# Attention weights of three batches transposed by VectorE and DMA instead of TensorE, in a fused attention and channel-mix kernel

## The chip, the cores and the metric

One core of a Trainium2 chip runs the whole program. The metric is the time of one execution on the device in microseconds. The kernel before took 440.34 us in the median of three runs, 440.08 to 441.02.

## What is computed

Sparse attention for 4 batches, 8 heads, 768 tokens and 64 features a head, and on its output a channel mix with a sigmoid gate. Each query sees the keys less than 16 tokens away and 24 summaries of 32 tokens each (maximum of the keys, mean of the values). Cut to what matters:

```
k_sum = k.reshape(B, H, nb, block, D).max(axis=3)
v_sum = v.reshape(B, H, nb, block, D).mean(axis=3)
scores_l = scale * q @ k.T, kept where |i - j| < 16
scores_s = scale * q @ k_sum.T + log(32)
a = softmax(concatenate([scores_l, scores_s]))
x = a @ concatenate([v, v_sum])

xk = mu_k * x + (1 - mu_k) * x_prev      # x_prev: x one token earlier
xr = mu_r * x + (1 - mu_r) * x_prev
out = sigmoid(xr @ w_r) * (relu(xk @ w_k) ** 2 @ w_v)
```

## The kernel before

Attention is cut into 32 units: a batch, one of four pairs of heads, and one half (`hf`) of the 768 tokens. `unit` (L515) plans one. TensorE (PE) makes the scores for each window of 64 queries against 96 keys and 24 summaries, 120 columns (L529). VectorE (DVE) adds the mask and finds the extreme (L539), ScalarE (ACT) takes the exponential (L543), and the rows are divided by their sums on ACT, DVE or GpSimd (POOL) (L560, L554, L565). The weights then stand with queries on the partitions, in tiles `y` of 128 x 3 x 120, one for each head of the pair. The product with the values needs them the other way round, with keys on the partitions. So PE transposes each tile with three instructions into the PSUM tile `pt` (L577), and ACT or DVE copies it into a tile `pts` of SBUF (L583, L585). The values follow on PE (L592), and ACT or DVE copies the result into `vx` (L607, L606).

The channel mix of a batch and half makes the two mixed inputs (L625 to L638), each split into a high and a low part, then the gate on PE (L679 to L681), and for each of eight slices of the hidden layer a first product (L708), rectified and squared (L714, L716, L718), and a second one (L733; the last slice is L759). The expert work of one batch is the long part on PE; the units of the next batch run among it. Batch 0's units have no such work beside them and stand at the start, with the loading and unpacking of the weights (L354 to L402). In the waits of the start PE multiplies zeros into a spare corner (L809).

All loads and stores are issued by SyncE (SP), in order: an issue that waits for its operands holds up all that stand behind it. Among them are the tokens of a batch for the means of its values (L420, into the tiles `st`, of which there are three, which the packed weights use too), the spreading of these means into the value tiles (L510), the queries (L518), keys (L439), values (L444) and the stores (L769).

What stands where is set by a table: `op` records every operation with the engines that could do it, what it reads and writes and an estimate of its length (`LENGTH`, L41). `ORDER` (L72) lists the operations by number, some with a letter for another engine than the first (D for DVE, A for ACT, P for POOL). `schedule` (L207) walks the table, gives each operation a buffer of its pool and an estimated start. Each engine runs its operations in that order. From the estimated starts comes the number of products of zeros. The buffers that matter here:

```
y=tiles("y", 4, [P, NSL, NK]), mn=tiles("mn", 4, [P, NSL]), sm=tiles("sm", 3, [P, 2 * NSL]),
rc=tiles("rc", 3, [P, 2 * NSL]), pts=tiles("pts", 2, [NK, NSL, P]),
...
st=tiles("st", 3, [P, 1024], U32), wc=tiles("wc", 4, [P, 512], U32),
sc=tiles("sc", 2, [P, NSL, P], pool=psum), pt=tiles("pt", 1, [P, 512], pool=psum),
```

A unit uses two `y`, two `pts`, and the one `pt` twice.

Of the kernel before, what the change touches and what calls it, by code (L numbers as in the profile page):

```python
# [21 lines left out]
P = 128  # L22
NPAIR = H // 2
NS = S // BLOCK
QW = 64
# [24 lines left out]
    wcast_p=650, mixa_p=560, kcopy_p=400, spread_p=800, norm3_p=1100, tiny=60, vzero=800, vzero_d=480,  # L50
# [13 lines left out]
MIX_PE = ()  # L64
NORM = "DVE", "POOL"
# [7 lines left out]
1 4 5 229 2 13 14 181 0 34 7 206 28 16 15 17 19 18 47 20 3 21P 53 182 72 231 35 36 189 191 193 185 190 186 194 38 37  # L73
187 183 39 40P 256 55 54 8 9 207 192 188 184 10 281 74 195 11P 214 216 210 212 196 218 29 217 198 30 208 31 197D 6 12
201 22 97 85 209 211 215 219 32D 23 202D 48 49P 204 24 213 199 50 25 220 200 221 26 279 56 51 222 57 203 52 223 58 76
75 224 59P 232 205A 33 225 377 77 226 305 241 78P 233 243 242 73 27 239 237 235 41 400D 66 378 257 401 244 238 234 240
42 236 227 43 44 264 268 402D 379D 260 266 262 269 245 246 258 45 60 261 267 247D 228 259 61 263 265 248D 380 403 249
230A 404P 254 282 250D 270 381 62 353 624 590 271 287 251 63 272D 393 64 65 291 289 252D 285 283 293 98 273 288 86 290
382 405 87 99 383 88 406D 384 253 276 294 79 286 255A 385D 407 100 292 306 80 277 81 329 284 274 82 394 295 67 1034
121 591 109 317 307 83 315 275 68P 311 313 296 309 308 408 298 386 278 297D 387 299 101 330 69 388 594 300 409 280A  # L80
301 648 91 650 599 89 316 318 314 310 335 336 339 333 337 331 395 389P 341 302 412P 410 312 110 390 70D 391D 354 71
303 392 413 396 90 111 414 332 122 415 411 340 338 319 102 416 112 320 123 103 321D 397 399 398 124 323 421 322D 133
# [12 lines left out]
766 1092 655 714 523D 524 525A 691 531 1039 1025 526 1040 822D 716 646 673 695 1043 677 738 719 678D 536 675 770 721
717 1095 534 537 693 1096 723 718 647A 725 844D 724 685 689 923 726 538 727 535 532 676D 696D 697 699D 741 924 679
1026 771 798 1030 1150 713 772 702 541 533 557 542 728 720 703 752 722 750 845 748 681 539A 925 729 846D 698 926 1029
823 730 700 558 824 559 701 548 742 744 746 747 745 749 774 704 1068 1151 743 826 751 825 731D 733 734 753 540 777
1153 775 732 1031 827 550 549 735 551 776 1154 785 552 754 555 564 778 736 1155 779 781 755 828D 756 560A 847 783 561
553 780 705A 757 829 784 782 758 737 739A 759D 1097 799 760 556 808 806 761 802 565D 804 810 809 786 787 566 807 803  # L100
562 852P 554 1035 563 800 853 788 1027 789P 854D 805 848P 811 567 801 790 1044 762 791 569 1045 830P 792 763A 793 570
1047 812 813 814D 855 1046 794 1049 1055 568 831 832D 815 795 797A 834 835 1051 1053 1050 818 849 836D 819 1052 577
574 571 816 1069 817 1048 820 833 837 575 1032 1070 1071 1033 1076 931D 850D 856 1074 1080 1072 578 1073 1081 1054
1056 1057 1077 1075 1078 572 857 1079 1082 1058 838 839 1059 1098 932 1060 858D 821 1101 1159 475 1094 1470 1478 576
840 842 1126 573 579 1480 1041 1468 1157 1594 1093 1036 1061 1062 1100 1474 1102 1063 841 851 859 927P 1064 843 1083
1085 1113 865 860 861 866 867 868A 862 1103 935D 1156 1469 936 1084D 1107 937D 938 1105 1111 928 1109 1086 1065 1127
1087D 863A 933 1597 1130 1088 879 1134 1136 1598 864 1099 1184 1536 1135 1106 1067 1114 1108 1110 1042 1472 1217 1132
934 869 880D 870 871 872 1540 1138 945D 1128 946 1089 1471 1539 873 874 877 1131 1112 929D 875 881 957 1137 1104 1139
876 930 1541 878 886 887D 884 1124 1133 1129 958 1115 1599 888 1140D 882 883 1116 1473 1482 953D 900 889A 1117 1118
1600 1481 1160 1090 901 1119 885 939 1161 1162 1120 1121 891 940 1167 1165 1475 890 892 893 898 954 1169 1163 894D 902  # L110
895 896 1171 1542 1141 1143 1122 1483 899 941 905 1142 903A 1091A 942 943 947D 904 959 955 956 960 944 1185 1123 1208
1210 948 897 1144 1152 1158 1242 1479 907 949 1145 950 951D 1192 952 1196 908 906 1146 961 1186 1194 1166 909 1197
1147 910A 1168 1125 1193 1270D 912 1182 1292 1271 1172 962D 963 911 980 913 1188 1272D 1187 1170 1212 1273 1293 1190
1191 1164 1484 1211 917 920 1173 1174 1213 1148 1214P 981D 1176D 1175D 918 1218 1189 982 964A 965 1476 1066 914 1195
1477 1486 1177 973 1178 915 1537 1216 1179 966 987 1225 983 1227 1219 921 1221 1603 1180 1222 1294 974D 1149A 1220
1228 1229 1230 1198 1223 984 1199 1201D 1200D 1243 1181 1487 1652 967 968 1224 975 1202 971 1209 916 919 1248 1203D
1204 969 972 1254 1246 1244 978 1226 1252 970 1245 1247 1255 988 1183A 1296D 1205D 979 1655 976A 1001 1231D 977 1232
# [139 lines left out]
def tile_kernel(ctx: ExitStack, tc: tile.TileContext, q, k, vT, v, fixed, w_k, w_v, w_r, out):  # L257
# [150 lines left out]
    def windows(vw):  # L408
        return vw.t[0:NK, 0:S].rearrange("p (w d) -> p w d", d=P)
# [498 lines left out]
```

## Time and profile before

| | |
|---|---|
| median of three runs | 440.34 us (440.08 to 441.02) |
| span of the profiled execution | 438.2 us; the page has no time of its own beside it |
| PE busy | 431.6 us, 3568 matmul records |
| VectorE busy | 295.4 us |
| ScalarE busy | 277.9 us |
| GpSimd busy | 31.1 us |
| DMA | 51.71 MB, 118 GB/s over the span |

The span is the time from the first to the last instruction of one execution; the time of a run has some more around it. Busy time of PE is modelled from records of pipelined instructions: two that follow each other overlap, so the sum of their durations is longer than the path through them. The chain of waits is a path through the run, followed back from the last instruction, and its pieces add up without overlap; what is on it has delayed the end. A stretch is a window of time counted from the start of the span. "SPq" is the queue of SyncE, on which a DMA is issued.

### The profile page before, as it was taken

The page shows a single profiled execution, that of the slowest core. Times are in us where ns is not written, and L with a number is a line of the kernel's source. Part 1 is how long each engine was busy: PE and PEld are TensorE (multiplying, and loading weights), DVE is VectorE, ACT ScalarE, POOL GpSimd, SP SyncE. Part 2 cuts the span into 40 slices and gives each one's busy share as a digit, 9 for nine tenths or more (in the row PEclk, how much of TensorE's full clock was granted, in tenths as well). Part 3 has the DMA queues.
Part 4 walks back from the last instruction along what each step waited for, and adds up shares of the span by engine and source line. Part 5 has one row for each costly group of instructions (what it writes and reads, how often), then busy time and mean ns, then how long its engine had stood idle before and what let it go on. Part 6 is the DMA issues. An engine that isn't in the chain of part 4 may idle for free.

```text
span 438.2 us, 9571 instructions
## 1 busy us (share of the span) xinstructions
PE 431.6 (99%) x3568; PEld 374.1 (85%) x3568; DVE 295.4 (67%) x961; ACT 277.9 (63%) x839; POOL 31.1 (7%) x69
## 2 busy tenths in 40 slices
PE   9999999999999999999999999999999999999996
PEld 8877988788887889889888888888888889889985
DVE  5999999998977877537667857456355754444121
ACT  4999999875998878557655767757445433223211
POOL 3322220100002000000010000000100000000000
PEclk9999999999999999999999999999999999999999
DMA  8979479457533584005361312102100010002003
GB/s 298 401 283 344 115 252 357 145 210 221 155 120 97 204 240 125 1 1 184 87 204 38 104 34 68 43 0 85 56 0 2 2 48 0 1 0 73 0 1 120
DMA packets 26878, 51.71 MB, mean 118 GB/s; under 512 B 2640, under 2 KB 14544, under 8 KB 26832
## 3 DMA queue, kind: packets, MB, share of 16 engines
q1 hardware_dynamic: 26832, 51.10, 35.2%
q8 instruction: 28, 0.46, 0.5%
q14 instruction: 18, 0.15, 0.1%
HBM read 43.03 MB, written 6.29 MB: 113 GB/s over the span
## 4 chain that ended last, share of the span: by engine, by line
PE 80%; ACT 7%; DMA 5%; DVE 4%; SPq 1%; issue 1%; DVEq 0%
PE mm L708 27%; PE mm L733 24%; PE av L592 5%; PE pt L577 4%; PE mm L681 4%; PE mm L680 4%; PE mm L679 4%; PE sc L529 4%; PE mm L759 4%; DMA st<-in_w_k 3%; DMA kt<-in_k 2%; ACT wc L361 2%; ACT y L543 1%; DVE y L539 1%; ACT L693 1%
## 5 line engine op out<-in xcount | busy, mean ns | idle before, releaser
L708 PE MATMUL mm<-xs,wk_h 128*128 128x384 f32 x512 | 101.9, 340 | 0.0
L708 PEld LDWEIGHTS mm<-xs,wk_h 128*128 128x128 f32 x512 | 90.0, 188 | 3.9 <-ACT r L714 0.3
L543 ACT ACTIVATE y<-y,mn 128x120 f32<-128x120 f32 x192 | 74.1, 388 | 20.7 <-DVE mn L539 20.3
L733 PE MATMUL mm<-wv_h,kh 128*128 128x512 f32 x168 | 67.4, 401 | 0.0
L733 PE MATMUL mm<-wv_l,kh 128*128 128x512 f32 x168 | 66.0, 393 | 0.0
L539 DVE CUSTOM_DVE_ANT_0 y<-sc,mask_sb 128x120 f32<-128x120 f32 x192 | 46.8, 275 | 22.0 <-PE pt L577 17.6
L718 ACT ACTIVATE r<-r 128x384 f32<-128x384 f32 x64 | 33.1, 521 | 40.9 <-DVE r L716 40.4
L708 PE MATMUL mm<-xs,wk_l 128*128 128x384 f32 x256 | 54.7, 334 | 0.0
L733 PE MATMUL mm<-wv_h,kl 128*128 128x512 f32 x168 | 48.7, 398 | 0.0
L708 PEld LDWEIGHTS mm<-xs,wk_l 128*128 128x128 f32 x256 | 45.3, 188 | 0.0
L723 DVE TENSOR_TENSOR kl<-r,kh 128x384 fp32r<-128x384 f32 x64 | 35.2, 553 | 14.4 <-ACT kh L722 12.2
L632 DVE SCALAR_TENSOR_TENSOR xa<-vx,fixed_sb,xa 128x384 f32<-128x384 f32 x64 | 39.1, 615 | 4.0 <-ACT xa L625 3.9
L638 DVE TENSOR_TENSOR xs<-xa,xs 128x384 fp32r<-128x384 f32 x64 | 34.4, 552 | 7.3 <-ACT xs L635 5.0
L679 PE MATMUL mm<-wr_h,xs 128*128 128x512 f32 x96 | 38.3, 399 | 0.0
L681 PE MATMUL mm<-wr_h,xs 128*128 128x512 f32 x96 | 37.6, 391 | 0.0
L680 PE MATMUL mm<-wr_l,xs 128*128 128x512 f32 x96 | 37.5, 390 | 0.0
L716 DVE TENSOR_SCALAR r<-mm 128x384 f32<-128x384 f32 x29 | 16.1, 554 | 31.4 <-PE mm L708 29.6
L733 PEld LDWEIGHTS mm<-wv_h,kh 128*128 128x128 f32 x168 | 31.5, 188 | 5.9 <-DVE kh L721 0.2
L543 ACT ACTIVATION_READ_ACCUMULATOR y<-y,mn 128x1 f32 x192 | 36.5, 190 | 0.0
L733 PEld LDWEIGHTS mm<-wv_l,kh 128*128 128x128 f32 x168 | 31.6, 188 | 5.5
L714 ACT ACTIVATE r<-mm 128x384 f32<-128x384 f32 x35 | 16.9, 485 | 30.1 <-PE mm L708 30.1
L733 PEld LDWEIGHTS mm<-wv_h,kl 128*128 128x128 f32 x168 | 30.6, 188 | 5.1
(87 smaller groups left out, 675.2 us busy)
## 6 DMA issues: line engine op xcount, KB each, us to landing
vx<-in_v SPq DMA_DIRECT2D x32, 384.0 KB
kt<-in_k SPq DMA_DIRECT2D x15, 544.0 KB
qt<-in_q SPq DMA_DIRECT2D x32, 192.0 KB
out<-z SPq DMA_DIRECT2D x23, 256.0 KB
st<-in_vT SPq DMA_DIRECT2D x12, 384.0 KB
st<-in_w_k SPq DMA_DIRECT2D x8, 512.0 KB
st<-in_w_v SPq DMA_DIRECT2D x8, 512.0 KB
st<-in_w_r SPq DMA_DIRECT2D x4, 512.0 KB
```

The source lines that it names most:

```text
L539: op("DVE", "mask", lambda h=h, i=i, var=var: nc.vector.tensor_tensor_reduce(out=y[h].t[:, i, :], in0=sc[h].t[:, i, 0:NK], in1=mask_sb[:, ...
L543: op("ACT", "exp", lambda h=h, i=i: nc.scalar.activation(y[h].t[:, i, :], y[h].t[:, i, :], AF.Exp, bias=mn[h].t[:, i:i + 1], scale=-1.0, a ...
L592: nc.tensor.matmul(av.t[hs, w * QW:(w + 1) * QW], windows(vw)[:, w, hs], pts[h].t[:, i, c * QW:(c + 1) * QW], start=True, stop=True,)
L632: op("DVE", "mixd", lambda xt=xt, xa=xa, p=p: nc.vector.scalar_tensor_tensor(out=xa.t, in0=xt.t[:, 1 + lo:1 + lo + HT], scalar=mu_sb[:, wh ...
L638: op("DVE", "sub", lambda xa=xa, xh=xh, xl=xl: nc.vector.tensor_tensor(out=xl.t, in0=xa.t, in1=xh.t.bitcast(F32), op=ALU.subtract), reads= ...
L679: nc.tensor.matmul(ps[t].t, xh.t[:, ts], wr_h[:, p, :], start=(p == 0), stop=False)
L680: nc.tensor.matmul(ps[t].t, xh.t[:, ts], wr_l[:, p, :], start=False, stop=False)
L681: nc.tensor.matmul(ps[t].t, xl.t[:, ts], wr_h[:, p, :], start=False, stop=(p == NPAIR - 1))
L708: nc.tensor.matmul(ps.t[:, 0:HT], w[:, j, p, :], x[p][s].t, start=(n == 0), stop=(n == 11))
L718: op("ACT", "square", lambda: nc.scalar.activation(r.t, r.t, AF.Square), reads=[(r, 0)], writes=[(r, 0)])
L723: op("DVE", "sub", lambda: nc.vector.tensor_tensor(out=kl.t, in0=r.t, in1=kh.t.bitcast(F32), op=ALU.subtract), reads=[(r, 0), (kh, 0)], wr ...
L733: nc.tensor.matmul(acc[t].t, a.t[:, t * P:(t + 1) * P], w[:, j, :], start=start, stop=stop)
```

## The change

For batches 1 to 3 (`BY_DMA`, 24 of the 32 units) the transposes on PE and the copies out of PSUM are gone. For each tile `y`, now 128 columns wide with 8 columns of zeros at the end of each third, VectorE turns every block of 32 x 32 within its place and writes the result into half of a tile `st`. This gives the right numbers within the blocks, with the blocks themselves still in rows by queries. Four DMAs (`away`) write the tile, 32 partitions each, to one of two buffers `dr` in DRAM, in pieces of 192 words, so that the blocks come to stand in their places; one DMA (`back`) reads it into a tile `pts` of 128 partitions that now holds both heads of a unit. There are still two tiles `pts`. The values read them in two runs of 32 columns. Batch 0 keeps the transposes on PE.

The order was searched anew for the whole program, so that operations change places and engines everywhere. Besides, the second half of the last piece of the experts (L796 and following) now waits for the first, and GpSimd clears the added columns of the four tiles `y` once.

```diff
-    wcast_p=650, mixa_p=560, kcopy_p=400, spread_p=800, norm3_p=1100, tiny=60, vzero=800, vzero_d=480,
+    wcast_p=650, mixa_p=560, kcopy_p=400, turn=500, spread_p=800, norm3_p=1100, tiny=60, vzero=800, vzero_d=480,
...
+BY_DMA = tuple((b, hf) for b in range(1, B) for hf in range(2))
+AWAY, BACK = (3 * 400, 600), (0, 300)
...
-1 4 5 229 2 13 14 181 0 34 7 206 28 16 15 17 19 18 47 20 3 21P 53 182 72 231 35 36 189 191 193 185 190 186 194 38 37
...
+834P 835 836D 837 1073 475 844D 577 578 845 854 1101 1102 1111 1109 1059 1061 1112 855 1107 1079 923P 1103 1104 761
...
-        y=tiles("y", 4, [P, NSL, NK]), mn=tiles("mn", 4, [P, NSL]), sm=tiles("sm", 3, [P, 2 * NSL]),
-        rc=tiles("rc", 3, [P, 2 * NSL]), pts=tiles("pts", 2, [NK, NSL, P]),
+        y=tiles("y", 4, [P, NSL, P]), mn=tiles("mn", 4, [P, NSL]), sm=tiles("sm", 3, [P, 2 * NSL]),
+        rc=tiles("rc", 3, [P, 2 * NSL]), pts=tiles("pts", 2, [P, 2 * NSL * P]),
...
+    pools["dr"] = [tc.dram_tile([P, 2 * NSL * P], F32, name=f"dr{i}") for i in range(2)]
...
+        if (b, hf) in BY_DMA:
+
+            st, dr = buf("st"), buf("dr")
+
+            def blocks():
+                return st.t[:, 0:2 * NSL * P].bitcast(F32).rearrange("p (j h i q) -> p j h i q", j=P // 32, h=2, q=32)
+
+            for h in range(2):
+                op("DVE", "turn", lambda h=h: nc.vector.transpose(
+                    out=blocks()[:, :, h].rearrange("p j i q -> p i j q"), in_=y[h].t.rearrange("p i (j q) -> p i j q", q=32)),
+                   reads=[(y[h], i) for i in range(NSL)], writes=[(st, h)])
+
+            def away():
+                for n in range(P // 32):
+                    nc.sync.dma_start(
+                        out=dr.t.rearrange("(j k) (n x) -> n k j x", k=32, n=P // 32)[n],
+                        in_=st.t[32 * n:32 * n + 32, 0:2 * NSL * P].bitcast(F32).rearrange("k (j x) -> k j x", j=P // 32))
+
+            op("SP", "away", away, reads=[(st, 0), (st, 1)], writes=[(dr, 0)], size=P * 2 * NSL * P * 4, more=AWAY)
+            op("SP", "back", lambda: nc.sync.dma_start(out=pts.t, in_=dr.t),
+               reads=[(dr, 0)], writes=[(pts, 0), (pts, 1)], size=P * 2 * NSL * P * 4, more=BACK)
+
+            def turned(h, i, c):
+                return pts.t[0:NK].rearrange("p (n h i q) -> p n h i q", n=P // 32, h=2, q=32)[:, 2 * c:2 * c + 2, h, i, :]
+        else:
...
+            def turned(h, i, c):
+                lo = (h * NSL + i) * P + c * QW
+                return pts.t[0:NK, lo:lo + QW]
...
-                        av.t[hs, w * QW:(w + 1) * QW], windows(vw)[:, w, hs], pts[h].t[:, i, c * QW:(c + 1) * QW],
+                        av.t[hs, w * QW:(w + 1) * QW], windows(vw)[:, w, hs], turned(h, i, c),
...
-        op("PE", "values", values, reads=[(vw, x) for x in "abc"] + [(pts[0], 0), (pts[1], 0)], writes=[(av, 0)])
+        op("PE", "values", values, reads=[(vw, x) for x in "abc"] + [(pts, 0), (pts, 1)], writes=[(av, 0)])
...
-                op("PE", "e2" if size == DM else "e2h", last, reads=[(kh, 0), (kl, 0), *w],
+                op("PE", "e2" if size == DM else "e2h", last, reads=[(kh, 0), (kl, 0), *w] + ([(acc[t], 0)] if part else []),
...
+        if o.name == "turn" and not padded:
+            padded = True
+            for t in pools["y"]:
+                nc.gpsimd.memset(t[:, :, NK:P], 0.0)
```

How the order moves is seen at three places; in the rows the lines of the changed kernel are its own (scores L533, values L628, second expert product L769).

On PE before, at a unit of batch 1: `sc` are its scores, `pt` a transpose of weights, `mm` gate products.

```order
L680 MATMUL mm_150<-wr_l,xs_123 128x512
L681 MATMUL mm_150<-wr_h,xs_126 128x512
L529 MATMUL sc_143<-kt_63,qt_67 64x120 x2
L529 MATMUL sc_144<-kt_63,qt_67 64x120 x2
L529 MATMUL sc_143<-kt_63,qt_67 64x120 x2
L529 MATMUL sc_144<-kt_63,qt_67 64x120 x2
L529 MATMUL sc_143<-kt_63,qt_67 64x120 x2
L529 MATMUL sc_144<-kt_63,qt_67 64x120 x2
L577 MATMUL pt_145<-ident_sb,y_89 120x128 x3
L679 MATMUL mm_150<-wr_h,xs_118 128x512
L680 MATMUL mm_150<-wr_l,xs_118 128x512
```

On PE now, at the first values of batch 1: `av` are the values of one unit, read from its fetched weights `pts`.

```order
L533 MATMUL sc_143<-kt_63,qt_65 64x120 x2
L533 MATMUL sc_144<-kt_63,qt_65 64x120 x2
L533 MATMUL sc_143<-kt_63,qt_65 64x120 x2
L533 MATMUL sc_144<-kt_63,qt_65 64x120 x2
L533 MATMUL sc_143<-kt_63,qt_65 64x120 x2
L533 MATMUL sc_144<-kt_63,qt_65 64x120 x2
L628 MATMUL av_146<-pts_103,vx_70 64x64 x12
L769 MATMUL mm_147<-wv_h,kh_132 128x512
L769 MATMUL mm_147<-wv_l,kh_132 128x512
```

The group of three transposes behind the scores is gone, and a large product stands right behind the values; over the batches 1 to 3 this happens 24 times, and happened twice before.

On SP before, in batch 1: only loads, the means (`vm`) and stores stand there.

```order
L510 DMA vx_72<-vm_83 24x6x128
L518 DMA qt_67<-in_q 128x384
L420 DMA st_137<-in_vT 128x768
L510 DMA vx_75<-vm_83 24x6x128
L518 DMA qt_66<-in_q 128x384
L420 DMA st_136<-in_vT 128x768
L439 DMA kt_64<-in_k 128x1088
```

On SP now, in batch 1: `dr<-st` is the sending of a unit's weights, `pts<-dr` the fetch.

```order
L590 DMA dr_154<-st_138 32x4x192 x4
L442 DMA kt_63<-in_k 128x1088
L513 DMA vx_74<-vm_83 24x6x128
L521 DMA qt_66<-in_q 128x384
L590 DMA dr_153<-st_137 32x4x192 x4
L595 DMA pts_104<-dr_153 128x768
L595 DMA pts_103<-dr_154 128x768
L423 DMA st_137<-in_vT 128x768
L590 DMA dr_153<-st_138 32x4x192 x4
L590 DMA dr_154<-st_136 32x4x192 x4
L805 DMA out<-z_106 128x512
L595 DMA pts_104<-dr_153 128x768
```

Hops now stand among the loads, some with the fetch right behind the sending that it needs, some two sendings together with other issues in between.

On VectorE before, in batch 1: `y_89,mn_94<-sc_144` is the mask, `pts_103<-pt_145` the copy of transposed weights.

```order
L539 ISA y_89,mn_94<-sc_144,mask_sb 128x120
L539 ISA mn_94 128x1
L723 TENSOR_TENSOR kl_135<-r_131,kh_133 128x384
L721 CAST kh_132<-r_130 128x384
L638 TENSOR_TENSOR xs_128<-xa_111,xs_129 128x384
L585 COPY pts_103<-pt_145 120x384
L473 TENSOR_TENSOR ks_81<-kg_78 128x24
```

On VectorE now, in batch 1: the block transposes of a unit's two tiles.

```order
L543 ISA y_90,mn_93<-sc_143,mask_sb 128x120
L543 ISA mn_93 128x1
L759 TENSOR_TENSOR kl_135<-r_130,kh_132 128x384
L584 STREAM_TRANSPOSE st_138<-y_92 128x3x4x32
L584 STREAM_TRANSPOSE st_138<-y_91 128x3x4x32
L668 SCALAR_TENSOR_TENSOR xa_112<-vx_77,fixed_sb,xa_112 128x384
L673 CAST xs_115<-xa_112 128x384
```

Two block transposes stand where copies out of PSUM did. Counted over the program, VectorE has 48 of them and 19 copies of `pts` fewer, 10 rectifications (L716) fewer and 13 first halves of the mix (L628) fewer; ScalarE has 29 copies of `pts` fewer and 10 rectifications more; GpSimd has 54 pieces of normalisation where it had 9. SP issues 96 sendings and 24 fetches more. The products of zeros are 55 instead of 49.

## Rows read from the trace of the kernel before

**Rows 1.** Page, busy time and share by engine; granted clock in 40 slices.
```profile
PE 431.6 (99%) x3568; PEld 374.1 (85%) x3568; DVE 295.4 (67%) x961; ACT 277.9 (63%) x839; POOL 31.1 (7%) x69
...
PEclk9999999999999999999999999999999999999999
```

**Rows 2.** Table by stretch, in us: busy by engine, then clock, DMA share, GB/s.
```profile
0.00:85.00 85.00, 82.39 (x887) 69.24 (x887) 77.56 (x272) 77.34 (x238) 21.08 (x44) 1.00 0.79 277
85.00:100.00 15.00, 15.00 (x98) 13.29 (x98) 14.81 (x37) 11.43 (x34) 0.00 (x0) 1.00 0.54 185
100.00:150.00 50.00, 50.00 (x560) 42.45 (x559) 41.86 (x164) 40.13 (x149) 4.29 (x10) 1.00 0.51 158
150.00:350.00 200.00, 199.97 (x1598) 174.29 (x1597) 127.00 (x422) 125.87 (x376) 5.73 (x15) 1.00 0.24 74
```

**Rows 3.** Waits of PE, longest first: total us, times, longest us.
```profile
PE av L809 <- POOL still L800: 1.0, 1, 1.0
PE sc L529 <- POOL kt L477: 0.4, 1, 0.4
```

**Rows 4.** Chain of waits from 85 to 434 us: shares by line.
```profile
by line: PE mm L708 34.3%; PE mm L733 29.8%; PE av L592 5.8%; PE pt L577 5.4%; PE mm L681 5.0%; PE mm L679 5.0%; PE mm L680 5.0%; PE sc L529 4.9%; PE mm L759 4.7%; PE pt L425 0.2%; issue 0.0%
```

**Rows 5.** Chain from 98 to 112 us: start us, us, what.
```profile
98.00 3.82 PE mm L708 x22
101.81 0.78 PE sc L529 x24
102.59 0.85 PE av L592 x24
103.44 0.47 PE pt L577 x3
103.91 1.39 PE mm L733 x6
105.30 0.33 PE pt L577 x3
```

**Rows 6.** The same from 376 to 384 us.
```profile
381.32 0.85 PE av L592 x24
382.17 1.59 PE mm L733 x6
```

**Rows 7.** Tile pt after 84 us: ns min/median/max, first and last start us.
```profile
L577 PE MATMUL pt<-ident_sb,y x141: 270/273/326, 85.7 to 349.8; 128*120 128x128 f32 x141
L583 ACT COPY pts<-pt x30: 455/478/483, 92.9 to 366.2; 120x384 f32<-120x384 f32 x30
L585 DVE COPY pts<-pt x17: 547/551/557, 111.4 to 347.8; 120x384 f32<-120x384 f32 x17
```

**Rows 8.** Timeline of PE, 5 to 12 us: start us, us.
```profile
6.58 3.17 PE L809 MATMUL av<-still 128*128 128x128 f32 x26
```

**Rows 9.** Groups of instructions of VectorE: busy us, mean ns, idle before.
```profile
L638 DVE TENSOR_TENSOR xs<-xa,xs 128x384 fp32r<-128x384 f32 x64 | 34.4, 552 | 7.3 <-ACT xs L635 5.0 <-PE mm L708 1.2 <-PE mm L680 0.9
...
L716 DVE TENSOR_SCALAR r<-mm 128x384 f32<-128x384 f32 x29 | 16.1, 554 | 31.4 <-PE mm L708 29.6 <-issue 1.7
...
L422 DVE TENSOR_REDUCE vs<-st 128x24 f32<-128x768 f32 x12 | 11.3, 941 | 0.0
...
L628 DVE TENSOR_SCALAR xa<-vx,om_sb 128x384 f32<-128x384 f32 x25 | 10.4, 417 | 2.7 <-issue 1.4 <-ACT vx L607 1.0
```

**Rows 10.** The same of GpSimd.
```profile
L565 POOL TENSOR_SCALAR y<-y,rc 128x120 f32<-128x120 f32 x9 | 5.1, 582 | 38.6 <-DVE mn L539 18.9 <-ACT y L543 17.3 <-DVE rc L551 2.5
```

**Rows 11.** Chain from 0 to 86 us: the DMAs that it waited for.
```profile
6.38 10.11 DMA kt<-in_k
...
34.26 7.79 DMA st<-in_w_k
...
72.31 5.79 DMA st<-in_w_k
```

**Rows 12.** Line L769 on SP's queue: issue ns min/median/max, first and last start us.
```profile
L769 SPq DMA_DIRECT2D out<-z x25: 332/423/1927, 101.2 to 435.2; - x25
```

More of the change, by code (lines that the diff above doesn't have):

```diff
@@ L78 @@
[L78 to L82, printed above, removed]
@@ L519, in unit @@
            writes=[(qt, 0)], size=P * HT * 4, more=(0, LATE if b else 0))
-        sc, y, mn, pts = [[buf(x) for _ in range(2)] for x in ("sc", "y", "mn", "pts")]
+        sc, y, mn = [[buf(x) for _ in range(2)] for x in ("sc", "y", "mn")]
+        pts = buf("pts")
         sm, rc, av = buf("sm"), buf("rc"), buf("av")
@@ L539, in unit @@
                 op("DVE", "mask", lambda h=h, i=i, var=var: nc.vector.tensor_tensor_reduce(
-                    out=y[h].t[:, i, :], in0=sc[h].t[:, i, 0:NK], in1=mask_sb[:, var, :], scale=-SCALE, scalar=3.0e38,
+                    out=y[h].t[:, i, 0:NK], in0=sc[h].t[:, i, 0:NK], in1=mask_sb[:, var, :], scale=-SCALE, scalar=3.0e38,
                     op0=ALU.add, op1=ALU.min, accum_out=mn[h].t[:, i:i + 1]),
@@ L554, in norm @@
                 nc.vector.tensor_tensor(
-                    out=y[h].t, in0=y[h].t, in1=rc.t[:, NSL * h:NSL * h + NSL].unsqueeze(2).broadcast_to([P, NSL, NK]),
+                    out=y[h].t[:, :, 0:NK], in0=y[h].t[:, :, 0:NK], in1=rc.t[:, NSL * h:NSL * h + NSL].unsqueeze(2).broadcast_to([P, NSL, NK]),
                     op=ALU.mult)
@@ L565, in norm_pool @@
                     nc.gpsimd.tensor_scalar(
-                        out=y[h].t[:, i, :], in0=y[h].t[:, i, :], scalar1=rc.t[:, NSL * h + i:NSL * h + i + 1],
+                        out=y[h].t[:, i, 0:NK], in0=y[h].t[:, i, 0:NK], scalar1=rc.t[:, NSL * h + i:NSL * h + i + 1],
                         scalar2=1.0, op0=ALU.mult, op1=ALU.mult)
@@ L571, in unit, with turn, source, there @@
                other=[x for x in (("DVE", "norm3", norm), ("POOL", "norm3_p", norm_pool)) if x[0] in NORM])
-        for h in range(2):
-            pt = buf("pt")
-            def turn(h=h, pt=pt):
-                for i in range(NSL):
-                    nc.tensor.transpose(out=pt.t[0:NK, i * P:(i + 1) * P], in_=y[h].t[:, i, :], identity=ident_sb)
-            def source(pt=pt):
-                return pt.t[0:NK, 0:NSL * P].rearrange("p (i c) -> p i c", c=P)
-            op("PE", "transpose", turn, reads=[(y[h], i) for i in range(NSL)] + [*IDENT], writes=[(pt, 0)])
-            op("ACT", "pts", lambda h=h, source=source: nc.scalar.copy(out=pts[h].t, in_=source()),
-               reads=[(pt, 0)], writes=[(pts[h], 0)],
-               other=("DVE", "pts_d", lambda h=h, source=source: nc.vector.tensor_copy(out=pts[h].t, in_=source())))
+        if (b, hf) in BY_DMA:
[17 more added lines that the diff above has]
+        else:
+            for h in range(2):
+                pt = buf("pt")
+                def turn(h=h, pt=pt):
+                    for i in range(NSL):
+                        nc.tensor.transpose(out=pt.t[0:NK, i * P:(i + 1) * P], in_=y[h].t[:, i, 0:NK], identity=ident_sb)
+                def source(pt=pt):
+                    return pt.t[0:NK, 0:NSL * P]
+                def there(h=h):
+                    return pts.t[0:NK, h * NSL * P:(h + 1) * NSL * P]
+                op("PE", "transpose", turn, reads=[(y[h], i) for i in range(NSL)] + [*IDENT], writes=[(pt, 0)])
+                op("ACT", "pts", lambda there=there, source=source: nc.scalar.copy(out=there(), in_=source()),
+                   reads=[(pt, 0)], writes=[(pts, h)],
+                   other=("DVE", "pts_d", lambda there=there, source=source: nc.vector.tensor_copy(out=there(), in_=source())))
+            def turned(h, i, c):
+                lo = (h * NSL + i) * P + c * QW
+                return pts.t[0:NK, lo:lo + QW]
```

148 lines of the change are left out of this document (77 added, 71 removed).

## The prediction

> **What bounds the kernel now.** I read the page's busy shares first: PE is busy for 99% of the span at a granted clock of 2.4 GHz throughout, VectorE for 67% and ScalarE for 63% [rows 1]. A busy PE can still be a waiting PE, so the next view is the table by stretch: from 85 us on PE has no idle time to speak of, while VectorE and ScalarE have some in every stretch but one; between 85 and 100 us VectorE is busy 14.81 of 15 us [rows 2]. The waits of PE say the same: the longest in the whole run is 1.0 us, at the very start [rows 3]. Then the chain of waits. Over the 349 us from 85 to 434 us it holds nothing but PE lines, and it gives each a share of the path, which busy time does not [rows 4]. In that stage a microsecond taken from PE is a microsecond of the kernel, as long as nothing else comes to be late. Before 85 us the chain also passes through weight loads [rows 11], and PE fills its idle time with products of zeros (L809).
>
> The sum is made against the profiled span of 438.2 us. The median of the runs is 440.34, so 2.1 us lie outside the span; I leave those as they are and count from 440.3.
>
> **What is removed from PE.** The chain gives the transposes (L577) 5.4% of 349 us [rows 4], 18.8 us for the 141 instructions that stand there, 47 groups of three [rows 7]. That is 0.40 us a group: 0.47 where it follows the values or the scores, 0.33 where it follows expert products [rows 5]. The mean duration of one transpose is 0.273 us [rows 7], but three in a row overlap, so durations would overstate the gain: 144 x 0.273 is 39 us. I take the path: 48 groups, 144 instructions, x 0.40 = 19.2 us.
>
> **What of it stays.** Part of those 0.47 us is the change from small products to large ones, and without the transposes the large ones stand right behind the values. One place of the trace shows that: values, then six expert products in 1.59 us, where six otherwise take 1.39 [rows 6, 5]. So the change itself costs 0.20 us. In the changed order of batches 1 to 3 a large product follows values or scores 24 times, and 2 times before: 22 x 0.20 = 4.4 us come back.
>
> **The values' new operand.** They now read the weights in two runs of 32 columns instead of one of 64. No row shows that. Twenty-four value matmuls stream 64 columns each in 0.85 us, twenty-four score matmuls 120 each in 0.78 [rows 5], so the number of columns does not set the time, and I take zero. The bounds are zero and a doubling of the streamed part, at most 24 units x 0.85 = 20.4 us; nothing speaks for a gain.
>
> **Filler at the start.** The changed order has 55 products of zeros against 49; the trace shows two passes for each (98), at 3.17 us / 26 = 0.122 us [rows 8]. Six more are 12 x 0.122 = 1.5 us in which the planner expected PE to be idle. The searched order also moves batch 0's units around; I allow 1.5 us either way for that, the size of the filler itself.
>
> **VectorE, ScalarE, GpSimd.** 48 block transposes of 128x384 come to VectorE. The trace has none. The nearest row is another pass of 128x384, 0.552 us; the upper bound is the dearest pass over a wide tile, 0.941 us [rows 9]; the lower is the 0.417 us of a one-operand pass [rows 9]. I take 0.55, since one instruction moves each element once: 26.4 us. Off VectorE go 19 of the copies out of PSUM (x 0.551 [rows 7] = 10.5), 10 of the rectifications (x 0.554 = 5.5) and 13 first halves of the token mix (x 0.417 = 5.4) [rows 9], with some smaller ones, so its total hardly moves. ScalarE loses 29 copies (x 0.478 = 13.9 us [rows 7]). GpSimd gets 45 more normalisation pieces at 0.582 us [rows 10], 26 us, and four small clears; it is busy for 7% of the span now. All of this is beside PE's work: cost nothing while the results arrive in time. The exception is the stretch around 85 to 100 us, where VectorE has no room; without that cover its added time is PE's.
>
> **The two hops through DRAM.** Each of the 24 units now sends 393 KB away in four DMAs and fetches them back in one: 120 issues, about 0.42 us each on SP's queue [rows 12], and 18.9 MB beside 51.7. The DMA engines were 79% busy up to 85 us, 51 to 54% from there to 150, 24% after [rows 2], so there is room where the hops stand. What a hop takes is bounded below by the last store, issued at 435.2 us and landed within the 438.2 us span, 3.0 us [rows 12], and above by loads the chain waited for, 5.8 to 10.1 us [rows 11]. I take 3.5 us, near the idle store. While the fetch waits for the sending to land, everything behind it on SP's queue waits: loads of q, k and v, the stores, the next unit's hops. A unit holds the queue for 4 x 0.42 + 3.5 + 0.42 = 5.6 us. The need is sharpest in batch 1. Between the values of its first and its eighth unit the changed order has on PE 108 products of 512 columns (x 0.232), 36 of 384 (x 0.174), six sets of scores (x 0.78) and seven of values (x 0.85) [rows 5]: 25.1 + 6.3 + 4.7 + 6.0 = 42 us, 6.0 us a unit. So 5.6 just fits, and the two tiles for the weights that come back let one unit's fetch run beside another's values. I cost the hops at nothing.
>
> **The sum.** 440.3 - 19.2 + 4.4 + 1.5 = **427.0 us**. Its own range is 423.5 (the filler costs nothing, 425.5, and 2 of the 4.4 us are hidden) to 431 (1.5 us for the start's order, and 2.5 us of new short waits, 0.1 us a unit).
>
> **The rivals.**
> (A) VectorE becomes late in batch 1. If a block transpose takes the 0.941 us of the dearest wide pass, the 16 of batch 1 add 16 x 0.39 = 6.2 us in a stage where VectorE was nearly full, and PE waits for them: 433 us. For it: 14.81 of 15 us busy [rows 2]. Against it: scores, rectifications and mixes were taken off VectorE in the same stage, and the dear row reads twice the columns. The Trainium skill ("VectorE: DVE Perf Modes", The three transpose paths, Rules for kernel authors) speaks against this change: a full 128x128 transpose goes to TensorE, and VectorE's blocks of 32x32 take 311 ns for such a tile. Three tiles would be an estimate of 0.93 us, about this rival's price, and 45 us over 48 instructions in place of 26; no run here shows it yet.
>
> (B) Slower: SP's queue becomes the bound. With sending at the 7.8 us of a loaded transfer [rows 11] a unit holds the queue for 4 x 0.42 + 7.8 + 0.42 = 9.9 us against the 6.0 us that PE gives it; over seven steps of batch 1 that is 27 us of waiting by the values, and 427 + 27 = 454. Waiting begins at a hold of 6.0 us and eats the whole gain of 13.3 at 6.0 + 13.3 / 7 = 7.9 us, a landing of 5.8. For it: loads landing in 5.8 to 10.1 us exist. Against it: they stand where the DMA engines are 79% busy, not half, and the order issues some pairs of sendings together, so that one wait serves two. The Trainium skill ("DMA: Bandwidth & Descriptors", Anatomy of one DMA) puts about 2 us of fixed cost on each DMA (for another issuing path), mostly the receipt of the write and heaviest to DRAM, plus bytes over 436 GB/s. For 393 KB that makes an estimate of 2.9 us, and hops that stay hidden; the 3.0 us of the last store agree.
>
> (C) The time saved on PE is given back on PE: the values with their cut operand, or a start that the new order makes longer. At half of the operand's bound, 10 us, that is 437; at the whole, 447. The cover of the column count speaks against it. That PE was not the bound at all has almost no chance with [rows 3].
>
> **How the numbers follow.** My forecast has 0.72, (A) 0.13, (B) 0.09, (C) 0.06. Runs of this kernel differ by 0.2%, 0.9 us, so less cannot be told from no change. Faster by more than that: the forecast, (A) and 0.01 of (C), together 0.86. Within it: 0.02 of (C), whose middle lies near 440. Slower: 0.12, (B) and the other 0.03 of (C). The range of 423.5 to 434 holds the forecast with its own bounds and (A), and leaves out (B), (C) and the edges.
>
> **What would show it.** Right: no transposes of weights on PE after batch 0, PE without waits after 85 us, the chain there all PE, and large products behind values longer by 0.20 us. The values still 0.85 us a unit. (A) shows as VectorE at 97% or more near 90 to 130 us and PE waiting for it or for what it feeds; (B) as PE waiting for the tile of fetched weights, with SP's queue held more than 6 us a unit; (C) as longer values or more filler. I am wrong if PE's waits after 85 us come to more than 4 us in all.

## The result and the profile after

The changed kernel takes 430.13 us (median of four runs, 429.75 to 430.3) against 440.46 (four runs beside it): ratio 0.976, 95% interval 0.975 to 0.978. That is 10.3 us faster; 13.3 were forecast, and the time lies inside the range. The profiled execution has a span of 428.5 us; that of before had 438.2.

The page of the changed kernel, busy time and share by engine, and the granted clock in 40 slices:

```profile
PE 419.4 (98%) x3436; PEld 360.8 (84%) x3436; DVE 302.5 (71%) x954; ACT 265.6 (62%) x791; POOL 64.9 (15%) x140
...
PEclk9999999999999999999999999999999999999999
```

PE has 12.2 us less and is still busy for 98% [rows 1]. VectorE rises by 7.1 us, ScalarE falls by 12.3, and GpSimd doubles to 64.9. DMA moves 70.60 MB, 18.9 more.

The table by stretch (us: busy by engine, then clock, DMA share, GB/s), as in [rows 2]:

```profile
0.00:85.00 85.00, 81.05 (x903) 68.46 (x904) 76.30 (x268) 75.33 (x233) 24.33 (x49) 1.00 0.73 261
85.00:100.00 15.00, 14.85 (x89) 12.05 (x88) 14.79 (x37) 12.23 (x36) 0.62 (x1) 1.00 0.92 311
100.00:150.00 50.00, 49.36 (x515) 41.22 (x514) 47.22 (x179) 38.66 (x149) 10.09 (x23) 1.00 0.79 240
150.00:350.00 200.00, 199.54 (x1530) 173.35 (x1529) 133.97 (x413) 118.11 (x335) 27.15 (x63) 1.00 0.46 142
```

Up to 85 us PE is idle for 3.95 us where it was idle for 2.61. From 100 to 150 us VectorE goes from 41.86 busy to 47.22, 94% of the stretch.

All waits of PE in the changed kernel (total us, times, longest us):

```profile
PE av L850 <- POOL still L836: 1.0, 1, 1.0
PE av L628 <- issue: 0.8, 2, 0.5
PE pt L606 <- ACT pts L615: 0.8, 2, 0.5
PE sc L533 <- POOL kt L480: 0.7, 1, 0.7
PE sc L533 <- DVE kt L480: 0.5, 1, 0.5
PE sc L533 <- DMA qt<-in_q: 0.5, 1, 0.5
PE av L628 <- ACT pts L615: 0.4, 1, 0.4
PE mm L769 <- DVE wv_l L405: 0.2, 1, 0.2
```

They come to 4.9 us. Behind 85 us stand two of these rows only, 0.2 us for a weight and 0.8 us in two waits ahead of the values (L628). "I am wrong if PE's waits after 85 us come to more than 4 us": they come to 1.0. Waits do not tell all, though: from 85 to 100 us PE counts as busy for 14.85 of 15 us, but with 89 matmuls where there were 98.

The chain of waits, from 102.7 to 424.5 us, by line, then five of its pieces (start us, us, what):

```profile
by line: PE mm L744 35.9%; PE mm L769 32.1%; PE av L628 6.4%; PE mm L715 5.3%; PE mm L717 5.1%; PE mm L716 5.1%; PE mm L795 4.8%; PE sc L533 4.8%; issue 0.3%; PE pt L428 0.2%; DVE z L801 0.2%
...
118.05 0.85 PE av L628 x24
118.90 2.31 PE mm L744 x12
...
121.21 0.78 PE sc L533 x24
121.99 0.85 PE av L628 x24
122.84 1.59 PE mm L769 x6
```

The transposes' 5.4% [rows 4] are gone, and nothing but PE's own lines took their place. The values take 0.85 us as before [rows 5]: the cut operand costs nothing. Large products right behind values are longer, as forecast: six take 1.59 us (1.39 elsewhere), twelve take 2.31 where [rows 5] give 12 x 0.174 = 2.08.

Ahead of 102.7 us the two chains differ. From 85 to 103 us, the chain of before and then that of the changed kernel, by line:

```profile
by line: PE mm L708 47.4%; PE mm L759 11.6%; PE mm L733 11.4%; PE sc L529 8.6%; PE mm L681 6.3%; PE mm L679 5.2%; PE mm L680 5.1%; PE pt L577 2.6%; PE av L592 2.4%; PE pt L425 0.6%
```

```profile
by line: DVE vs L425 14.8%; DVE xs L674 12.5%; issue 12.3%; DVE xa L668 8.8%; DVE kl L759 8.3%; DVE wv_l L405 6.7%; DVE st L584 5.4%; DVE kg L468 4.8%; DVE y L543 4.8%; DVE wc L382 4.7%; DVE wk_l L405 3.4%; DVE z L801 3.3%; DVE xs L673 3.1%
```

Before, all of it was PE. Now it is VectorE, with the block transposes (`st L584`) at 5.4%. A busy share of 14.81 before and 14.79 now does not tell these apart; the chain does.

The new instructions: block transposes, sendings and fetches (ns min/median/max, first and last start us).

```profile
L584 DVE STREAM_TRANSPOSE st<-y x48: 537/576/581, 84.8 to 347.9; 128x384 f32<-128x384 f32 x48
```

```profile
L590 SPq DMA_DIRECT2D dr<-st x96: 302/442/1607, 88.5 to 352.3; - x96
L595 SPq DMA_DIRECT2D pts<-dr x24: 333/342/457, 94.7 to 354.5; - x24
```

A block transpose takes 0.576 us; 0.55 was taken. SP's queue waited for a sending to land 20 times, 1.0 us each, 3.5 at most:

```profile
SPq L595 <- DMA dr<-st: 20.2, 20, 3.5
```

### The profile page after: what moved, and what is told of

Its sections match the earlier page's. It is cut to its first block, busy times and chain, and to the rows that moved or that the text cites. A ratio compares the mean times of both kernels' runs of the same rounds, so it can differ in the third digit from the quotient of the medians.

```text
span 428.5 us, 9550 instructions
## 1 busy us (share of the span) xinstructions
PE 419.4 (98%) x3436; PEld 360.8 (84%) x3436; DVE 302.5 (71%) x954; ACT 265.6 (62%) x791; POOL 64.9 (15%) x140
## 2 busy tenths in 40 slices
DMA packets 44160, 70.60 MB, mean 165 GB/s; under 512 B 4560, under 2 KB 28752, under 8 KB 44112
## 4 chain that ended last, share of the span: by engine, by line
PE 77%; ACT 9%; DVE 7%; DMA 3%; issue 2%; SPq 0%; POOL 0%; DVEq 0%; ACTq 0%
PE mm L744 27%; PE mm L769 24%; PE av L628 5%; PE sc L533 4%; PE mm L715 4%; PE mm L717 4%; PE mm L716 4%; PE mm L795 4%; ACT y L547 2%; DMA kt<-in_k 2%; ACT wc L364 1%; DMA st<-in_w_k 1%; ACT pts L615 1%; ACT y L564 1%; PE av L850 1%
## 5 line engine op out<-in xcount | busy, mean ns | idle before, releaser
L769 PE MATMUL mm<-wv_h,kh 128*128 128x512 f32 x168 | 66.6, 396 | 0.0
L769 PE MATMUL mm<-wv_l,kh 128*128 128x512 f32 x168 | 66.0, 393 | 0.2 <-DVE wv_l L405 0.2
L769 PE MATMUL mm<-wv_h,kl 128*128 128x512 f32 x168 | 48.0, 394 | 0.0
L750 ACT ACTIVATE r<-mm 128x384 f32<-128x384 f32 x45 | 21.8, 485 | 42.0 <-PE mm L744 36.8
L664 POOL TENSOR_SCALAR xa<-vx,om_sb 128x384 f32<-128x384 f32 x26 | 19.3, 742 | 174.7 <-DVE kh L757 35.8
L674 DVE TENSOR_TENSOR xs<-xa,xs 128x384 fp32r<-128x384 f32 x64 | 35.5, 560 | 9.4 <-ACT xs L671 8.3
L716 PE MATMUL mm<-wr_l,xs 128*128 128x512 f32 x96 | 37.4, 390 | 0.0
L769 PEld LDWEIGHTS mm<-wv_h,kh 128*128 128x128 f32 x168 | 31.5, 188 | 6.9 <-DVE kh L757 0.6
L769 PEld LDWEIGHTS mm<-wv_l,kh 128*128 128x128 f32 x168 | 31.5, 188 | 6.5 <-DVE wv_l L405 0.6
L769 PEld LDWEIGHTS mm<-wv_h,kl 128*128 128x128 f32 x168 | 31.0, 188 | 6.6 <-DVE kl L759 0.4
```

Source lines behind the costliest of these rows:

```text
L674: op("DVE", "sub", lambda xa=xa, xh=xh, xl=xl: nc.vector.tensor_tensor(out=xl.t, in0=xa.t, in1=xh.t.bitcast(F32), op=ALU.subtract), reads= ...
L716: nc.tensor.matmul(ps[t].t, xh.t[:, ts], wr_l[:, p, :], start=False, stop=False)
L750: op("ACT", "relu", lambda: nc.scalar.activation(r.t, ps.t[:, 0:HT], AF.Relu), reads=[(ps, 0)], writes=[(r, 0)], other=("DVE", "relu_d", l ...
L769: nc.tensor.matmul(acc[t].t, a.t[:, t * P:(t + 1) * P], w[:, j, :], start=start, stop=stop)
```

## How far the start is behind

PE runs the same products in nearly the same sequence, so its progress at one moment can be compared. Products done at 102.75 us, from the table by stretch with one source line at a time; the line of the first expert products stands here for before and after.

```profile
0.00:102.75 102.75, 24.94 (x132) 22.88 (x132) 1.00 0.74 260
```

```profile
0.00:102.75 102.75, 22.47 (x121) 20.82 (x121) 1.00 0.76 267
```

| done by | 85 us, before | after | 102.75 us, before | after |
|---|---|---|---|---|
| first products (0.174 us each) | 84 | 84 | 132 | 120, the 121st just begins |
| second products (0.232) | 54 | 45 | 63 | 63 |
| last slice (0.232) | 0 | 0 | 9 | 6 |
| gate (0.232) | 60 | 56 | 72 | 72 |
| scores (0.033) | 244 | 264 | 288 | 288 |
| values (0.035) | 192 | 192 | 199 | 192 |

At 85 us the changed kernel is 9 x 0.232 + 4 x 0.232 - 20 x 0.033 = 2.4 us behind; at 102.75 us 12 x 0.174 + 3 x 0.232 + 7 x 0.035 = 3.0 us. From there before needs 335.45 us and the changed kernel 325.75, 9.7 less with 3.0 more to do: the part behind 103 us saves 12.7 us.

The kernel before had by then also done transposes that the change spares: one group of three by 85 us and two by 102.75 us, 0.40 us each. So the new order lost 2.8 us up to 85 us, and 3.8 us up to 102.75 us.

## The experiments

Each ratio is to the kernel before, run beside it, with its 95% interval. The sum explains the gain; the runs below ask whether the gain is PE's transposes, what the hops and the block transposes cost, and where the start lost its time.

**Transposes back on PE.** Three idle transposes ahead of the values of each DMA unit and three behind, results unused; all else as changed.

```diff
+        def idle_turn():
+            for _ in range(NSL):
+                nc.tensor.transpose(out=pools["pt"][0][:, NSL * P:NSL * P + P], in_=ident_sb, identity=ident_sb)
         def values():
+            if (b, hf) in BY_DMA:
+                idle_turn()
...
+            if (b, hf) in BY_DMA:
+                idle_turn()
```

> The changed kernel, with six transposes of a constant added on PE to each of the 24 units of batches 1 to 3, three in front of the values and three behind; nobody reads them, the hops stay. Theory (the gain is PE's transposes, at 0.33 to 0.47 us a group on the path, less the 0.20 us that the change to large products costs anyway): 24 x (0.33 + 0.47 - 0.20) = 14.4 us more than the 430.1 of the changed kernel, 442 to 449 us. Rival (the gain came from the order searched anew, or from copies taken off the other engines): within 3 us of 430.1.

446.24 us, ratio 1.013 (1.011 to 1.016): 16.1 us above the changed kernel. PE had no wait over 1.0 us. Large products again follow transposes, so the switch comes off, and the sum gives 19.2 - 4.4 = 14.8 us; 16.1 is measured. On this run's chain from 85 to 440 us the 48 groups hold 6.2% of 355 us, 0.46 us each where the sum has 0.40, which is more than the 1.3 us between them. The new order alone does not carry the gain; the instructions taken off PE do.

**No hops.** Sending and fetch emit nothing, so the DMA units multiply old weights; the block transposes still run.

```diff
-            op("SP", "away", away, reads=[(st, 0), (st, 1)], ...
+            op("SP", "away", lambda: None, reads=[(st, 0), (st, 1)], ...
-            op("SP", "back", lambda: nc.sync.dma_start(out=pts.t, in_=dr.t),
+            op("SP", "back", lambda: None,
```

> The changed kernel without the sendings and fetches of batches 1 to 3: 120 DMAs and 18.9 MB less, and no wait of the values for them. The values read what batch 0 left in the two tiles, so the weights of batches 1 to 3 do not reach the output. Theory (the hops are hidden behind PE's other work): 429 to 430.5 us. Rival (the 3 us by which the kernel is slower than the forecast are waits for the hops or what SP's queue holds up): 426 to 428 us.

429.73 us, ratio 0.975 (0.972 to 0.978): 0.4 us below the changed kernel, less than the interval. 120 DMAs of 18.9 MB cost nothing that can be told from zero, as the prediction took them.

**Each fetch twice**, for all units, for batch 1 alone, and for batch 3 alone.

```diff
-            op("SP", "back", lambda: nc.sync.dma_start(out=pts.t, in_=dr.t),
+            op("SP", "back", lambda: [nc.sync.dma_start(out=pts.t, in_=dr.t) for _ in range(2)],
```

(For one batch the range is `1 + (b == 1)` or `1 + (b == 3)`.)

> The changed kernel with each of the 24 fetches made twice, the second behind the first into the same tile. A unit's hold of SP's queue grows by a landing and an issue, by the estimate from rows of before 3.5 + 0.4 us, from 5.6 to 9.5 us against 6.0 us a unit that PE gives in batch 1. If SP's queue is as near its limit as that sum says: 27 x (9.5 - 6.0) / 3.9, about 24 us more, 440 to 455 us. If the order leaves room (fetches stand behind other issues, two sendings together): under 4 us more, 430 to 434 us.

> The changed kernel with the fetch made twice in batch 1 alone, eight units. With all 24 the time rose by 34 us. Theory (SP's queue binds where units follow each other every 6.0 us, in batch 1): at least half of the 34 us, 446 to 462 us. Rival (a longer hop costs the same in any batch): a third of it, about 442 us.

> The same in batch 3 alone, where the values of two units stand 9 us or more apart on PE. Theory (there SP's queue has room): 430 to 433 us. Rival (a longer hop costs the same in any batch): about 442 us.

| | us | ratio | above the changed kernel |
|---|---|---|---|
| all | 464.80 | 1.056 (1.052 to 1.061) | 34.7 |
| batch 1 | 454.49 | 1.034 (1.031 to 1.038) | 24.4 |
| batch 3 | 432.22 | 0.981 (0.978 to 0.985) | 2.1 |

With all doubled, SP's queue waits 3.2 us for each first copy, and PE waits for fetched weights and for what stands behind them. SP's queue, then the waits of PE:

```profile
SPq L595 <- DMA pts<-dr: 77.6, 24, 6.5
```

```profile
PE av L628 <- DMA pts<-dr: 14.4, 6, 4.3
PE av L628 <- DMA vx<-vm: 8.2, 3, 3.8
PE sc L533 <- DMA qt<-in_q: 4.4, 4, 2.6
```

Both single batches came as expected; all together cost more than the 440 to 455 us expected from SP's queue alone. So rival (B)'s mechanism is real, and its place is batch 1: one more landing a unit turns the gain into a loss there, while in batch 3 it costs 2.1 us (four runs, 429.82 to 433.07). Batch 2 alone was not run; 8.2 us of the 34.7 are left for it and for what the batches do to each other. With all doubled the waits above are 27.0 of the 34.7 us; the granted clock fell too (last section).

**Fillers only in the first 12 us of the plan**; all later products of zeros are left out.

```diff
-            for _ in range(many if used[quiet] + 300 < end else 0):
+            for _ in range(many if used[quiet] + 300 < end and o.start < 12000 else 0):
```

> The changed kernel with the products of zeros left out from the third batch of them on, so that PE idles where it filled. Theory (they stand in time in which PE would wait anyway): 429.5 to 430.7 us, the granted clock unchanged. First rival (they delay real work): 428 to 429 us. Second rival (an idle PE loses its clock for a while): the granted clock falls in the first 40 us and the time is over 431 us.

430.37 us, ratio 0.979 (0.975 to 0.982); in the profiled run, of 430.13 us, the clock is at 1.00 in every stretch shown above. Up to 85 us PE is busy for 76.44 us there in place of 81.05, and the time is the same. So the fillers stand in idle time. Two of the six runs took 433.31 and 433.48 us, though, with a mean granted clock of 0.983 and 0.987; the others had 0.988 to 0.998, and all four of the changed kernel 0.998 or more. So the second rival came in part: without the fillers the clock falls in some runs. Where in a run it falls was not seen. The 1.5 us that the prediction put on six more of them is no cost of theirs; it is idle time of the new order, which they only show.

**Block transposes twice, and nearly none.** Each written twice; or one column of 32 of each, so that the units multiply weights that were mostly not turned.

```diff
-                op("DVE", "turn", lambda h=h: nc.vector.transpose(
-                    out=blocks()[:, :, h]..., in_=y[h].t...),
+                op("DVE", "turn", lambda h=h: [nc.vector.transpose(
+                    out=blocks()[:, :, h]..., in_=y[h].t...) for _ in range(2)],
```

```diff
+                op("DVE", "turn", lambda h=h: nc.vector.transpose(
+                    out=blocks()[:, 0, h, 0], in_=y[h].t[:, 0, 0:32]),
```

> The changed kernel with each of the 48 block transposes made twice, 48 x 0.574 = 27.6 us more on VectorE. Theory (VectorE binds only up to about 103 us, where five of the 48 stand; behind that its work lies beside PE's): about 5 x 0.5 = 2.5 us of it reaches the end, 431 to 434 us. Rival (VectorE is near its limit throughout batches 1 to 3): 436 us or more.

> The changed kernel with each block transpose cut to one block column of 32 (the rest of the tile is sent as it lies there, so the weights of batches 1 to 3 are not what the output needs): about 48 x 0.45 = 22 us less on VectorE. Theory (VectorE binds up to about 103 us, PE after): 428 to 429.7 us, at most the five transposes that stand before 103 us. Rival (what the kernel lacks to the forecast of 427.0 is the price of the block transposes): 427 or less.

Twice: 446.54 us, ratio 1.015 (1.012 to 1.017), 16.4 us above. My theory fell: 27.6 us more on VectorE were not hidden. PE lost time beyond the start, in batch 1 and in batch 2 (table by stretch):

```profile
85.00:100.00 15.00, 14.15 (x86) 11.66 (x85) 14.60 (x37) 11.04 (x30) 0.74 (x4) 1.00 0.85 278
100.00:150.00 50.00, 44.91 (x447) 36.29 (x447) 47.40 (x165) 36.50 (x141) 8.44 (x21) 1.00 0.68 200
150.00:250.00 100.00, 95.34 (x825) 78.69 (x823) 84.09 (x273) 59.63 (x194) 16.01 (x37) 1.00 0.63 197
```

From 100 to 150 us VectorE stood at 47.22 of 50 us and now stands at 47.40: it had hardly any room, and the added work pushed PE instead. From 150 to 250 us it rises from 75.18 us to 84.09 of 100, and PE still falls from 99.54 to 95.34: a share over 100 us does not show where the room is missing. The chain from 85 to 250 us does, with the block transposes now its largest line:

```profile
by line: DVE st L584 14.8%; PE mm L770 8.7%; PE mm L745 7.8%; DVE y L543 6.5%; issue 6.2%; DMA qt<-in_q 4.1%; ACT y L547 4.0%; DVE xa L669 3.6%; PE sc L533 3.4%; PE av L629 3.1%; DVE kl L760 2.7%; PE mm L716 2.4%; PE mm L796 2.4%; ACT y L56
```

The rival was right for batches 1 and 2; from 250 to 350 us, among batch 3's units, PE was idle for 0.85 us only.

Nearly none: 428.67 us, ratio 0.974 (0.972 to 0.977), 1.5 us below, as expected of them. What is left of each still takes 0.207 us, so 0.37 us went and not 0.45, and 1.5 us is less than their whole price. The chain from 85 to 103 us is PE's again:

```profile
by line: PE mm L744 43.8%; PE mm L769 22.7%; PE mm L795 7.7%; PE mm L715 7.6%; PE mm L716 7.6%; PE mm L717 7.6%; PE sc L533 4.3%
```

Its progress at 85 us is that of the changed kernel (45 second products, 56 of the gate), and at 102.75 us it is six or seven first products ahead, 1.0 to 1.2 us. So the block transposes put VectorE on the path from 85 to 103 us, for 1.0 to 1.5 us, and what is lost by 85 us is not theirs.

**Relief of VectorE.** Four pieces of weight unpacking to GpSimd; those and three casts to ScalarE; the four and, besides, a load of tokens and one of keys issued ahead of the first sending. The changed kernel ran again beside the first two.

```diff
-139 141D ... 143D ... 165D ... 173D
+139 141P ... 143P ... 165P ... 173P
```

```diff
-511D ... 507D ... 515D
+511 ... 507 ... 515
```

```diff
-661 619 507D ... 764 633
+661 507D ... 764 619 633
```

> The changed kernel once more, unaltered, as the common mark for the two runs beside it. Both theories: 429.5 to 430.5 us, ratio to the kernel before 0.975 to 0.978.

> Two casts of weights and two byte conversions that VectorE does before 103 us are given to GpSimd; nothing else moves. Theory: the change lost about 3.4 us in the start and up to 103 us because VectorE is the last to be ready there, so about 1.7 us taken off VectorE gives back 0.5 to 2 us: 428 to 429.7 us. Rival: the start is bound by loads or by ScalarE, or GpSimd's slower pieces come late themselves: the same as the unaltered changed kernel beside it to within 0.5 us, or slower.

> The same, and three more casts go from VectorE to ScalarE. Theory: up to 1 us below the run with GpSimd alone (427.3 to 429.5 us), as long as ScalarE, which is 12.2 us of 15 busy from 85 to 100 us, does not come late in VectorE's place. Rival (ScalarE bounds the start): 0.5 to 2 us above the run with GpSimd alone.

> The kernel with four pieces on GpSimd, and besides the first load of the tokens for batch 1's means, with the key load after it, issued on SP's queue before the first unit's weights are sent away, not behind them. In the run with the four pieces alone the chain from 85 to 97 us went from the block transposes through the four issues of the first sending (0.33 to 0.45 us each) to that load (3.20 us) and on to VectorE. Theory: this was the second cover that was short there, so the two edits together give back 0.7 to 2 us of the changed kernel's 430.4: 428.4 to 429.7 us, ratio to the kernel before 0.972 to 0.9765, and the sending is gone from the chain there. Rival: a third thing stands as late (the three tiles that these loads share, VectorE itself): 429.8 to 431 us, ratio 0.977 to 0.979, and the chain names it.

| | us | ratio |
|---|---|---|
| changed kernel again | 430.63 | 0.977 (0.975 to 0.980) |
| four pieces to GpSimd | 429.95 | 0.978 (0.975 to 0.981) |
| and three casts to ScalarE | 434.78 | 0.987 (0.985 to 0.990) |
| the four, and the load first | 431.01 | 0.978 (0.977 to 0.980) |

The ratios go by all runs: with the four pieces on GpSimd four of six lie between 429.45 and 429.99 us, two at 431.81 and 434.56. None is faster than the changed kernel by more than the intervals. Three casts more on ScalarE cost 4.8 us against the four pieces alone, beyond the rival's 0.5 to 2: from 85 to 100 us VectorE is then idle for 4 us and PE waits, with ScalarE's exponentials and casts on the chain. The table by stretch, then the chain from 85 to 103 us:

```profile
85.00:100.00 15.00, 12.65 (x76) 9.90 (x76) 10.98 (x30) 11.39 (x30) 1.53 (x3) 1.00 0.88 290
```

```profile
by line: PE mm L744 13.6%; ACT y L547 9.1%; PE mm L769 7.9%; issue 7.8%; ACT xs L671 7.4%; ACT L547 7.1%; PE mm L795 7.1%; PE mm L717 5.1%; PE mm L715 5.1%; PE mm L716 5.1%; DVE wv_l L405 3.9%; DVE xa L668 3.5%; ACT z L729 3.3%; ACT wc L364
```

The first relief did not tell my theory from its rival, and its profile says why: the four pieces lay before 85 us. VectorE falls from 76.30 to 75.08 us there, and from 14.79 to 14.59 in the stretch that binds. Its chain from 85 to 97 us shows a second cover that is short, the sending:

```profile
88.31 0.50 DVE st L584
...
88.87 0.33 SPq L590
...
89.25 0.43 SPq L590
...
89.72 0.45 SPq L590
...
90.21 0.44 SPq L590
...
90.77 3.20 DMA st<-in_vT
```

The load of tokens waits behind the four issues. With that load first (the last run) the sending is off the chain, and VectorE alone is on it again, with the same 14.8% of `vs L425` and 12.5% of `xs L674`, up to the same 102.7 us; the time is unchanged:

```profile
by line: DVE vs L425 14.8%; DVE xs L674 12.5%; issue 11.1%; DVE xa L668 10.8%; DVE wv_l L405 10.5%; DVE kl L759 7.8%; DVE st L584 5.4%; DVE y L543 4.8%; DVE kg L468 4.8%; DVE wk_l L405 3.4%; DVE z L801 3.3%; DVE xs L673 3.1%; DVE y L558 3.0
```

The rival was right: behind one short cover stands the next.

## Why the prediction was right, and where it was off

**Direction and mechanism: right.** PE was the bound from 102.7 us on, the transposes came off its path, the large products behind values cost their 0.20 us, the values cost nothing, and nothing came to be late there beyond 0.8 us. The sign "the chain there all PE" failed from 85 to 102.7 us, where the chain is VectorE's. Transposes back on PE cost 16.1 us where the sum has 14.8.

**Size: 10.3 us and not 13.3.** By the two profiled spans it is 9.7, so 3.6 us are to be found:

- **"Filler at the start"** was the mis-sized term. I took 1.5 us, which with the two groups of transposes spared by 102.75 us would have the changed kernel 1.5 - 0.8 = 0.7 us behind there. It was 3.0: 2.3 us more, beyond the 1.5 us that I allowed for the start's order. By 85 us it was 2.4 behind: PE has 1.3 us more idle time and twelve more passes of zeros (1.5 us), less 0.4 us for one spared group. From there to 102.75 us another 1.0 us was lost, less 0.4 us for the second group. The filler without which the time is the same was the sign, not the cause. What in the new order of batch 0 costs the 2.8 us up to 85 us was not tried and stays open.
- **"Cost nothing while the results arrive in time"** named the exception of 85 to 100 us and then put no price on it. It was 1.0 us by the products done at 102.75 us, which are part of the 3.0, and 1.5 us by the time of the run with nearly no block transposes.
- **Waits of the values** behind 103 us: 0.8 us, inside the 2.5 that the range had for short waits.
- The part behind 103 us saved 12.7 us; 46 x 0.40 - 4.4 - 0.8 = 13.2 were to be had. The last 0.5 us stay open.

**VectorE.** A block transpose took 0.576 us against 0.55, so (A) did not come at its price of 0.941 us and 6.2 us. Its mechanism did come, at 1.0 to 1.5 us: VectorE is busy for 12.76 of 13 us from 90 to 103 us and ends the chain there; over all of 90 to 130 us it is at 37.94 of 40, 95% and not 97. The Trainium skill ("VectorE: DVE Perf Modes", The three transpose paths, Rules for kernel authors) gives 311 ns for a 128x128 tile of bf16, and three of these an estimate of 0.93 us; this trace, with fp32 and three tiles in one instruction, does not agree, and its number decides. But I had priced (A) too low: with 0.576 us more in each the kernel takes 16.4 us more, not hidden in batch 2 either. Going by proportion, an estimate, 0.93 us would have cost 16.4 x 0.35 / 0.576 = 10 us, and the whole gain. The cost need not go by proportion, as nearly no block transposes gave back only 1.5 us; but by this estimate (A) meant about no gain, and not the 433 us that I gave it.

**The hops.** Hidden, as costed, but not by the working. I held a unit's hop at 5.6 us of SP's queue, 3.5 of them for the sending to land, and counted nothing else there. The waits for sendings come to 20.2 us over 24 fetches, 0.84 us each. Sendings in pairs are not the whole reason: at 252.67 us a fetch stands right behind its own sending, whose last issue ends at 251.08, and starts 1.6 us later. So a hop holds the queue for 4 x 0.44 + 0.84 + 0.34 = 2.9 us. The other issues take 16.4 us between 103.4 and 148.8 us, where seven units are sent and seven fetched: 2.3 us a unit, an estimate from these issues alone, without the queue's other waits. Together that is 5.2 us, close to the 5.6 by luck: one term too long and one left out. With 3.2 + 0.34 us more for a second fetch it is 8.7 us against the 6.0 a unit that PE was to give, which fits batch 1's loss. A landing of 3.2 us for 393 KB, in stretches of that run with the DMA engines 47 to 85% busy, is near the 3.5 taken. The Trainium skill ("DMA: Bandwidth & Descriptors", Anatomy of one DMA) gives an estimate of 2.9 us; the 3.2 us of this trace are near that too. (B) did not come, but the doubled fetches put its margin at less than one landing a unit.

**(C)** came in part: not longer values, but a start that the new order makes longer, at 2.3 us and not 10.

## What to carry to other kernels

Work taken off a full engine is worth its time on the chain, not its durations, and it returns that only while the engine that takes it over has room in that very stretch: VectorE at 71% of the span stood at 94% where it counted, and twice the work cost 16.4 us. When an order is searched anew, compare progress product by product at one moment: the start's loss shows there and in no single wait. Before moving work to relieve an engine, check that the piece lies in the stretch where that engine ends the chain, and what stands next behind it.

## What was not expected of the hardware

The clock. In the run with batch 1's fetches doubled the granted clock (third number from the end) drops where PE has waited:

```profile
130.00:135.00 5.00, 4.85 (x44) 3.83 (x42) 4.22 (x14) 4.68 (x18) 0.73 (x1) 1.00 0.33 105
135.00:140.00 5.00, 0.04 (x2) 0.07 (x3) 3.02 (x15) 0.78 (x4) 0.00 (x0) 0.94 0.67 220
140.00:145.00 5.00, 5.00 (x35) 4.88 (x36) 1.65 (x5) 1.45 (x6) 1.06 (x3) 0.50 0.66 202
145.00:150.00 5.00, 5.00 (x21) 3.93 (x19) 2.82 (x5) 2.42 (x6) 0.57 (x2) 0.88 0.81 255
```

PE is idle from 135 to 140 us; then, busy again, it runs at 0.50, the 1.2 GHz level, before 2.4 GHz come back. So a wait on fetched weights costs more than its length: 15.9 us of such waits in that run went with 24.4 us of time; how much of the rest is the clock's was not separated. The few idle pieces that the changed kernel has left its clock at 1.00; without the later products of zeros it fell below 0.99 in three runs of six.

A block transpose lasts 0.576 us in the record, but 0.48 to 0.50 on the chain: its record is 0.08 to 0.10 us longer than what it holds up.
